# A work list and its loads, ordered anew from the value products of batch 2 on

## The chip, the cores and the metric

The kernel runs on one core of one Trainium2 chip. The metric is the device time of one execution in microseconds (us). Five engines work side by side, each on its own in-order queue: TensorE (PE, matrix products), VectorE (DVE), ScalarE (ACT), GpSimd (POOL) and SyncE (SP). An engine meets other engines' work only at semaphores. POOL, SP and ACT also issue DMAs, which move data while the engines go on.

## The reference

A causal attention over 8 batches, 8 heads, 576 queries and 64 channels, with 16 extra "beacon" keys and values that every query sees, and behind it a gated feed-forward block on the 4,608 rows that come out:

```python
scores = scale * np.matmul(q, k_all.transpose(0, 1, 3, 2))     # k_all: 16 beacons, then 576 keys
scores = np.where(causal, -1000000000.0, scores)
a = np.exp(scores - scores.max(-1, keepdims=True))
a /= a.sum(-1, keepdims=True) + 1e-09
x = np.matmul(a, v_all)                                        # then heads side by side: 4608 x 512
g = x @ w_gate
out = ((g * (1.0 / (1.0 + np.exp(-g)))) * (x @ w_val)) @ w_out   # d_ff = 1536
```

## The kernel before

Nothing is scheduled by a loop. One long string, `plan`, is the order of all work: each letter is one piece of work, `piece()` turns it into instructions on the engines concerned, and each engine takes its instructions in that order. The n-th letter of a kind is always the same piece, so a new order of letters changes only when a piece is issued. The list has 1,742 letters.

- `T`, `K`, `Q`: turn the keys and queries of batches 0 to 2 on PE and copy them into `kT` and `qT`.
- `l`: the next DMA load of the list `loads` (119 of them), issued by POOL. `vl[b][i]` is a chunk of the values of batch b (0: 16 beacon rows, 1: 112 rows, 2 to 4: 128 rows, 5: 80 rows), `kl[b][i]` the same for keys, `ql[b][i]` a chunk of queries (128 rows, the last 64). From the 25th on, a load first waits until PE has finished the last piece but one ahead of it (`passed[-2]`). `vb` and `qk` have two buffers each, taken by batch in turn. So a value load waits for the last value product of the batch two before, and a key or query load for the DMA transpose that read its place.
- `t`: one DMA transpose, issued by SP, from `qk` into `kT` or `qT` (batches 3 to 7, ten each: key chunk, query chunk, in turn). Written here as "the key transpose of batch 4, chunk 2".
- `S`: scores of one of four units A to D of a head pair on PE; `E`: the exponent on ACT; `D` or `M`: the causal mask of one unit, on DVE or on POOL.
- `P`, `p`: the value products of a head pair, first and second half, on PE; `R`: normalisation on DVE. "P 2.3" is batch 2, head pair 3.
- `V`: when the four head pairs of a batch are normalised, five or six DMA transposes on SP put them into `xT` (V 2 is that of batch 2).
- `G`, `H`: gate and value products of one of 12 column blocks of a chunk of 512 tokens on PE (16 matmuls in all); `a`: tanh on ACT; `1`, `2`: two operations on DVE that end in `hT`. There are nine chunks, j = 0 to 8; "G 2.0" is chunk 2, block 0. Chunk 2 needs V 2, chunk 3 needs V 3, and so on.
- `F`: output products on PE, 24 letters for 256 rows; `O` or `o`: the copy out of PSUM on DVE or ACT, and the store, which SP issues.

PSUM has four slots. A piece of PE that starts a new result takes the slot that has been free longest, and waits for the `E`, `2`, `R` or `O` that freed it. SP's queue holds the transposes `t` and `V` and the stores; POOL's holds loads and masks.

In the profile most PE work has line L151, the matmul in the helper `halves`; the full-height value products of batches 0 to 3 have L465; the DMA transposes are L320 (`t`) and L519 (`V`); loads are L202; exponents L379; masks L388 (DVE) and L392 (POOL).

Of the kernel before, what the change touches and what calls it, by code (L numbers as in the profile page):

```python
# [70 lines left out]
def kernel(  # L71
# [134 lines left out]
    def q_loads(b):  # L206
        return [lambda c=c, n=n: rows(natural(b, 0), q, b, c, 0, P * c, n) for c, n in enumerate((P, P, P, P, 64))]
# [455 lines left out]
    for i in range(2):  # L663
# [7 lines left out]
    vl = [v_loads(b) for b in range(B)]  # L671
    kl = [k_loads(b) for b in range(B)]
    ql = [q_loads(b) for b in range(B)]
# [17 lines left out]
    def piece(kind):  # L691
# [69 lines left out]
        "SH2EHDta1Gal2Gl1SH2ElHaMl1Gal2G1SH2ElHaDlG1a2lG1lSHE2HaMl1Ga2FFH1l2FaFlFF1FFFlF2FPplFRPlFFpVFlRF",
        "FFFFlFFFFFloFFFoFFlFFFFFFlSPESFlpEMSFRFESlFFFFEMDSFlFFEDSFFPlEGMoDpolGRHlGal1Hl2Ga1SlHE2HlaDG1al",
        "2G1SHEt2HaDt1Ga2Gt1SH2EtHMa1tGa2Gt1SH2EtHaD1Gta2G1tSH2EtHaDS1Pa2Ep1SlFEFRFFFlSFEF2VSFlFDFEFFMDSP",
        "ESlFpESFRMFEFlSFFESMDFFDlFFEDSFFFEMSFFFoMFFFoFFFESFFPEMSFtpEDGRMtGSHtEHMat1Ga2FtFH12Gta1Gt2HGta1",
        "Ht2Ha1Gta2FFH12Ga1G2FFFSFEFFFHOMGoaSHE1H2aDGa1G12H2SHaE1FFF2aFMP1Pp2pRFlSFEFFFRSlFESFFDPVlESDFpE",
        "MSFRlFFESFMFFElSFFFESMFFFOFElSFFOMFESMFFMFEDSFFFEMSFPEMFPpMpRGFRGHGa1H2Ha1Ga2FFH12Ga1G2HGa1H2Ha1",
        "Ga2FFH12Ga1G2HGa1H2Ha1Ga2FFF1SFEF2FHoDSOFaFFEF1SFF2EFSFDFFEDSFFPEMSFpEDSFRFESFFFDPEVMSFpEDSFREFS",
        "FFFEDMSFFOFESFDFFoFDFFESFFFEMSPFEDSpFERFMFFFFMFFFFFPOGOpGRHGa1H2Ga1H2Ga1H2Ga1H2Ga1PH2paGRH1VGa2H",
        "1G2a1FFFF2FHGa1H2Ha1Ga2FFH12FaFG1G2HGa1H2FaFFG1F2FFFFFFFFFFFFoFFFoFFFFFFFFHGa1FFFF2HGa1H2FaH1Ga2",
        "FF1G2FFFFHGa1H2FaHOGOa1G1H2Ha2G1a2G1H2Ga1FFFF2FFHGa1H2Ha1Ga2FFF1G2FFFHGa1FFH2Ha1Ga2FFH12Ga1G2FFF",  # L770
# [45 lines left out]
```

## Time and profile before

| what | value |
|---|---|
| median of 3 runs | 370.32 us (369.93 to 370.75) |
| the profiled execution | 369.36 us |
| its span, first to last instruction | 367.6 us |
| PE busy | 355.6 us, 97% |
| DVE, ACT, POOL busy | 227.1, 185.9, 124.6 us |
| granted TensorE clock, mean | 0.999 |
| DMA, mean over the span | 108 GB/s |

How to read it: spans are from the first to the last instruction, and the execution's own time is 1.76 us longer. Busy times of different engines overlap. Engines wait for each other through semaphores, and a wait in the profile is put down to whatever ended last before it; where that engine had long been done, it was something else. The chain of work that ended last goes back from the last instruction through whatever released each step.

### The profile page before, as it was taken

Reading aid. Unit: us, or ns where it says so; the run is one execution under the profiler, and the core shown is the slowest. Engines: PE = TensorE matmul, PEld = TensorE weight load, DVE = VectorE, ACT = ScalarE, POOL = GpSimd, SP = SyncE. Lnnn points to the kernel's source line nnn. Section 1 sums busy time; section 2 is a strip of 40 time slices with the busy share of each in tenths; the row PEclk is TensorE's granted clock in tenths of the full one; section 3 lists DMA queues with packets and bytes.
Section 4 is the critical chain, followed back from the end, with each engine's and each line's share of the span. In section 5 each row is a group of like instructions: output and inputs, shape, how many; then the busy total and the mean of one; then the engine's idle time right before and its main releaser. Section 6 shows DMA issues by size and latency. Waiting matters only on the chain.

```text
span 367.6 us, 11647 instructions
## 1 busy us (share of the span) xinstructions
PE 355.6 (97%) x5037; PEld 219.9 (60%) x5037; DVE 227.1 (62%) x429; ACT 185.9 (51%) x276; POOL 124.6 (34%) x201
## 2 busy tenths in 40 slices
PE   7799999989999999999999999999999999999996
PEld 3588565655565555555665567556766555555554
DVE  4577786548764676277636683767568735766631
ACT  3874688953576651736774458237913322322201
POOL 8862456972366286770350027000200000000000
PEclk9999999999999999999999999999999999999999
DMA  8999999999999999999598309301330201100113
GB/s 147 162 193 201 204 164 160 147 170 176 158 127 176 175 115 107 112 201 150 63 180 101 86 7 124 67 0 59 68 116 14 54 13 46 60 3 0 60 59 114
DMA packets 143988, 39.88 MB, mean 108 GB/s; under 512 B 130368, under 2 KB 139328, under 8 KB 143936
## 3 DMA queue, kind: packets, MB, share of 16 engines
q0 software_dynamic: 95424, 18.85, 73.0%
q1 hardware_dynamic: 48224, 19.92, 30.1%
q8 instruction: 39, 0.64, 0.7%
q10 hardware_dynamic: 288, 0.36, 0.3%
q14 instruction: 13, 0.11, 0.1%
HBM read 38.27 MB, written 9.44 MB: 130 GB/s over the span
## 4 chain that ended last, share of the span: by engine, by line
PE 88%; DMA 4%; DVE 3%; ACT 2%; issue 1%; POOL 1%; SPq 1%; POOLq 0%; ACTq 0%
PE gv_ps L151 51%; PE o_ps L151 23%; PE s_ps L151 6%; PE pv_ps L151 4%; PE pv_ps L465 4%; DMA xT<-x 2%; DMA qk<-in_q_dram 2%; PE t_ps L283 1%; ACT p L379 1%; DVE x L494 1%; SPq L519 1%; DVE x L427 0%; DVE kT L246 0%; POOL qk L193 0%; DVE p L388 0%
## 5 line engine op out<-in xcount | busy, mean ns | idle before, releaser
L151 PE MATMUL gv_ps<-xT,wg 64*128 64x512 bf16 (+2 forms) x912 | 196.0, 365 | 2.2 <-DVE p L388 1.9
L151 PE MATMUL gv_ps<-xT,wv 64*128 64x512 bf16 (+2 forms) x912 | 197.2, 365 | 0.0
L379 ACT ACTIVATE p<-s_ps 128x832 bf16<-128x832 f32 (+2 forms) x127 | 104.2, 867 | 36.8 <-PE s_ps L151 35.3
L551 ACT ACTIVATE th<-gv_ps 128x512 f32<-128x512 f32 (+2 forms) x114 | 65.5, 574 | 112.1 <-PE gv_ps L151 111.2
L151 PE MATMUL o_ps<-wo,hT 64*128 64x512 bf16 (+2 forms) x912 | 113.9, 365 | 0.2
L556 DVE SCALAR_TENSOR_TENSOR u<-th,gv_ps 128x512 f32<-128x512 f32 (+2 forms) x114 | 74.9, 657 | 59.3 <-ACT th L551 59.0
L151 PEld LDWEIGHTS <-wg 64*128 64x128 bf16 x912 | 83.9, 94 | 41.4 <-issue 1.9
L151 PEld LDWEIGHTS <-wv 64*128 64x128 bf16 x912 | 83.6, 94 | 35.2 <-issue 0.5
L563 DVE SCALAR_TENSOR_TENSOR hT<-gv_ps,u 128x512 bf16<-128x512 f32 (+2 forms) x114 | 75.2, 663 | 3.6
L151 PEld LDWEIGHTS <-hT 64*128 64x128 bf16 x912 | 46.7, 94 | 30.0 <-PE o_ps L151 1.2
L392 POOL TENSOR_SCALAR_AFFINE_SELECT p<-p 128x256 bf16<-128x256 bf16 (+2 forms) x66 | 25.3, 405 | 74.6 <-ACT p L379 72.3
L151 PE MATMUL s_ps<-qT,kT 64*128 64x336 bf16 (+3 forms) x512 | 45.0, 250 | 2.2 <-DVE kT L246 0.5
L202 POOL DMA_DIRECT2D vb<-in_v_dram x40 | 34.0, 854 | 22.7 <-PE gv_ps L151 15.9
L151 PEld LDWEIGHTS <-kT 64*128 64x128 bf16 x512 | 25.2, 94 | 21.9 <-DVE kT L246 1.2
L388 DVE TENSOR_TENSOR p<-p,upper 128x256 bf16<-128x256 bf16 (+2 forms) x77 | 21.4, 298 | 22.3 <-ACT p L379 21.2
L494 DVE TENSOR_TENSOR x<-pv_ps,rec 128x640 bf16<-128x640 f32 (+1 forms) x32 | 25.3, 791 | 1.2
L202 POOL DMA_DIRECT2D qk<-in_q_dram x25 | 21.3, 852 | 11.0 <-PE pv_ps L465 3.5
L246 DVE COPY o_sb<-o_ps 128x512 f32<-128x512 f32 (+2 forms) x22 | 14.0, 663 | 17.8 <-PE o_ps L151 12.8
L202 POOL DMA_DIRECT2D qk<-in_k_dram x25 | 21.1, 844 | 9.3 <-PE s_ps L151 3.9
L493 DVE RECIPROCAL rec<-pv_ps 128x10 f32<-128x10 f32 (+1 forms) x32 | 6.9, 215 | 24.2 <-PE pv_ps L151 16.2
L151 PEld LDWEIGHTS <-p 64*128 64x128 bf16 x960 | 18.4, 94 | 3.4 <-DVE x L494 0.2
L244 ACT ACTIVATE o_sb<-o_ps 128x512 f32<-128x512 f32 (+2 forms) x16 | 8.7, 570 | 22.5 <-PE o_ps L151 21.7
(63 smaller groups left out, 136.6 us busy)
## 6 DMA issues: line engine op xcount, KB each, us to landing
out_dram<-o_sb SPq DMA_DIRECT2D x34, 256.0 KB, 3.4
vb<-in_v_dram POOLq DMA_DIRECT2D x24, 128.0 KB, 7.1
qk<-in_q_dram POOLq DMA_DIRECT2D x20, 128.0 KB, 6.4
qk<-in_k_dram POOLq DMA_DIRECT2D x15, 128.0 KB, 6.8
wv<-in_moe_w_val_dram POOLq DMA_DIRECT2D x4, 384.0 KB, 8.9
wg<-in_moe_w_gate_dram POOLq DMA_DIRECT2D x4, 384.0 KB, 8.7
wo<-in_moe_w_out_dram POOLq DMA_DIRECT2D x2, 768.0 KB, 15.1
qk<-in_k_dram POOLq DMA_DIRECT2D x2, 576.0 KB, 13.4
```

The source lines that it names most:

```text
L151: ins = nc.tensor.matmul(o, lhsT=l, rhs=r, start=start, stop=stop)
L202: return nc.gpsimd.dma_start(dst[p0 : p0 + n, c, :, 0:D], src[b, :, r : r + n, :].rearrange("h j d -> j h d"))
L244: nc.scalar.activation(o, i, ACT.Copy)
L246: eng.tensor_copy(o, i)
L379: nc.scalar.activation(p_of(b, m, u == "A")[:, :, c0 : c0 + w], ps[:, :, 0:w], ACT.Exp, scale=0.125)
L388: nc.vector.tensor_tensor(out=ap, in0=ap, in1=upper[:, None, d : d + w].to_broadcast([P, 2, w]), op=ALU.mult)
L392: nc.gpsimd.affine_select(out=ap, in_=ap, compare_op=ALU.is_ge, fill=0.0, base=d, pattern=[[0, 2], [1, w]], channel_multiplier=-1,)
L465: ins = nc.tensor.matmul(o_ps[:, side, 68 * c : 68 * c + D + 1], lhsT=pt[n % NPT][:, side, col : col + P], rhs=vb[b % 2][:, t, 2 * m + sid ...
L494: nc.vector.tensor_tensor(out=xs[b][:, c0:NKT, P * m : P * m + P].rearrange("p c (h d) -> p h c d", d=D), in0=o[:, :, :, 0:D], in1=rec[:, ...
L551: nc.scalar.activation(th[:, 0:w], gvs[n][:, 0, 0:w], ACT.Tanh, scale=0.5)
L556: nc.vector.scalar_tensor_tensor(out=u[:, 0:w], in0=ths[n][:, 0:w], scalar=1.0, in1=gvs[n][:, 0, 0:w], op0=ALU.add, op1=ALU.mult)
L563: nc.vector.scalar_tensor_tensor(out=hTs[j][:, f, c0:c1], in0=gvs.pop(n)[:, 1, 0 : c1 - c0], scalar=0.5, in1=ths.pop(n)[:, 0 : c1 - c0], o ...
```

## The change

Up to letter 380 of the list (PE reaches it at 72.4 us) and up to the 54th load nothing is changed. Behind it the remaining 1,362 letters and 65 loads are put into a new order. The counts of every kind stay, with one exception: one causal mask moves from POOL (`M`) to DVE (`D`).

What moves, in the order of the list:

- P 2.3 and p 2.3 stand right behind P 2.2 and p 2.2 and ahead of the gate products of chunk 1, instead of behind them.
- V 2 stands between the transposes of batch 3 and those of batch 4, instead of behind those of batch 4. Chunk 2's gate and value products follow chunk 1's at once, and the 48 output letters of rows 512 to 1023 come behind them instead of ahead.
- The value products of batch 3 move from there to behind chunk 2, in pairs: P 3.0 with P 3.1, P 3.2 with P 3.3.
- The remaining loads are mixed over batches and kinds. Three early ones of the values of batches 4 and 3 and the end of batch 4's keys and queries go first, then none over more than 20 gate and value letters, and then 14 in close order, which begin with `ql[6][4]` and end with `vl[3][4]` and `vl[3][5]`.
- From there on stages keep their order, with value products, stores and transposes shifted by some letters. At the end, the last four copies out of PSUM swap engines two and two (`Oo` and `oO`).

```diff
@@ -678,11 +678,11 @@
         run_loads(2)[1], run_loads(2)[0], vl[2][5], ql[3][0], vl[1][5], kl[3][1], vl[1][3], lambda: load_wo(1),
         kl[3][2], vl[2][4], vl[2][3], vl[2][0], vl[2][2], vl[2][1], kl[3][0], ql[3][1], kl[3][3], ql[3][2],
         kl[3][4], ql[3][3], kl[3][5], ql[3][4], kl[4][0], kl[4][1], ql[4][0], kl[4][2], ql[4][1], kl[4][3],
-        ql[4][2], kl[4][4], ql[4][3], kl[4][5], ql[4][4], vl[3][0], vl[3][1], vl[3][2], vl[3][3], vl[3][4],
-        vl[3][5], kl[5][0], kl[5][1], ql[5][0], kl[5][2], ql[5][1], kl[5][3], ql[5][2], kl[5][4], ql[5][3],
-        kl[5][5], ql[5][4], vl[4][0], vl[4][1], vl[4][2], vl[4][3], vl[4][4], vl[4][5], kl[6][0], kl[6][1],
-        ql[6][0], kl[6][2], ql[6][1], kl[6][3], ql[6][2], kl[6][4], ql[6][3], kl[6][5], ql[6][4], vl[5][0],
-        vl[5][1], vl[5][2], vl[5][3], vl[5][4], vl[5][5], kl[7][0], kl[7][1], ql[7][0], kl[7][2], ql[7][1],
+        ql[4][2], kl[4][4], ql[4][3], vl[4][3], vl[3][0], vl[4][4], kl[4][5], ql[4][4], ql[6][4], kl[6][4],
+        vl[4][1], vl[3][2], vl[3][1], vl[3][3], vl[4][2], kl[5][1], ql[5][0], ql[6][3], vl[4][5], kl[5][0],
+        vl[3][4], vl[3][5], ql[5][3], kl[6][2], ql[6][0], kl[5][5], ql[6][1], ql[5][1], kl[5][2], vl[5][0],
+        kl[6][1], ql[5][4], kl[5][3], kl[5][4], kl[6][5], vl[5][1], vl[4][0], kl[6][0], ql[5][2], kl[6][3],
+        ql[6][2], vl[5][2], vl[5][3], vl[5][4], vl[5][5], kl[7][0], kl[7][1], ql[7][0], kl[7][2], ql[7][1],
         kl[7][3], ql[7][2], kl[7][4], ql[7][3], kl[7][5], ql[7][4], vl[6][0], vl[6][1], vl[6][2], vl[6][3],
@@ -754,22 +754,22 @@
         "lqKGlQSlHElGDa1lSHE2HaD1Gal2SHE1s2aFFFDESF1FFEls2EDSlTETlKlTKqlTDqKlksQEQSESPEDpSRPEplDSRESlFFFD",
-        "ESlFDFFEDSPlpEDlsRFEFSlFFDFElSPEDtlpSlRFESFtFlFFDESDFFVlFEDFSOFFlESOFFFlESPplESRFFlESFFFElSFFFEM",
-        "SFFFMESFMFFMESFtMDFFESPMDtMpoDPEOlpRlSGEtlRMGtDHlGat1Ht2Gal1Ht2Gat1Hl2Gta1Ht2lGa1Ht2Gat1H2Gtla1H",
-        "t2Ga1StHE2HMat1Gal2tG1SHt2EHaDl1SFaFFl2EFFF1SFMESF2FFlFEDSFPEMpPDlRpSFEFRVSFFFESlFDFFESlFFFESFMF",
-        "OlFESFFOFMFESPlEpSlRFESFFMFMFDESlFtPEMDpSRFtMESFlFFEFMDGtDGtSHEtFFaMGl1tFF2FFFtSHOEHaMtol1Ga2G1t",
...
+        "ESlFDFFEDSPlpEDlsRFEFSlFFDFElSPEDtlpSlRFESFtFlFFDESDFFVlFEDFSOFFlESOFFFlESPplESRFFlESFFFElSFMMFM",
+        "FESMFFMDFESFtMFMESFFFEMtSPOpEMOSREMPtpDRPptRGltGlHtGat1H2Gat1H2VGal1Hl2Gal1H2Ga1H2Ga1SHtE2HaDtG",
+        "1a2tG1SHEt2HaDt1Ga2Gt1SH2EtHaMtG1a2Gt1SHE2tHaD1Ga2G1SH2EHMa1Gla2Gl1SlH2ElHal1Ga2lG1lSH2ElHalG1al",
+        "2G1MSHME2lHaDl1Gal2Gl1SHl2EHDal1SFaFF2lEFFF1SFlESF2FlFFDEFPMpMPRplSFRlEFSFFEFFDSFESMFtFFFEDSFFOF",
+        "EFSFDFoMFFFESFtFFEDSFPtEMpPRMptSlFREFSFlFEFFDVSlFEFDFFFSMFESlFOFFFEOSlFFDFEFlFFFlFSFESMDFFFFEMFF",
...
```

More of the change, by code (lines that the diff above doesn't have):

```diff
@@ L761 @@
[L761 to L770, printed above, removed]
@@ L771 @@
-        "FFFFFFOFFFHOGa1H2Ha1Ga2FFH12Ga1FFFF2FFHFaFFF1FFFF2FFFFFOFFFFOFFFFFFFFFFFFFFFFFFFFoFFOFFFFFFFFFOo",
-        "FFFFFFFFFFFFoO",
+        "ESlFDFFEDSPlpEDlsRFEFSlFFDFElSPEDtlpSlRFESFtFlFFDESDFFVlFEDFSOFFlESOFFFlESPplESRFFlESFFFElSFMMFM",
+        "FESMFFMDFESFtFMFESMFFFEMtSPOpEMOSREMPtpDRPptGRltGlHtGat1H2Gat1H2VGal1Hl2Gal1H2Ga1H2Ga1SHtE2HaDtG",
+        "1a2tG1SHEt2HaDt1Ga2Gt1SH2EtHaMtG1a2Gt1SHE2tHaD1Ga2G1SH2EHMa1Gla2Gl1SlH2ElHal1Ga2lG1lSH2ElHalG1al",
+        "2G1MSHME2lHaDl1Gal2Gl1SHl2EHDal1SFaFF2lEFFF1SFlESF2FlFFDEFPMpMPRplSFRlEFSFFEFFDSFESMFtFFFEDSFFOF",
@@ new lines @@
+        "EFSFDFoMFFFESFtFFEDSFPtEMpPRMptSlFREFSFlFEFFDVSlFEFDFFFSMFESlFOFFFEOSlFFDFEFlFFFlFSFESMDFFFFEMFF",
+        "FFlFFMFtFoFlFFOFFFlFFFGlGlHlGa1FlFH2lHa1Gtla2FFF1tG2FFtFPFFptFRFFHtGa1H2FaHOGOa1Gl2H1lGa2Hl12Gal",
+        "1SHEl2HaDlG1a2Gl1SHlE2HaDl1SFaFlF2EFFF1SlFEtP2FMFpMtFRFFSPEtFSpMESFRtFEFSFFDPEDtSFpEDStFRlFESMFF",
+        "FEDVSlFFFoFDPloFFpElSFRFESFMFFlESFPMESFplESFRFMFFEMFFMFDSFtESFPEFMtSpFEDGRtGOHDoGat1H2Gta1Ht2Ga1",
+        "Ht2Gat1SHE2tHMa1Gat2G1tSH2EHtaD1Gat2G1StH2EHaDG1a2G1SHE2HaM1FaSFF2EFFF1SMFESF2FFFEMSFPEDFFpMSFRl",
@@ new lines @@
+        "ESFFFEFDVSlFFESDPlFFEpMFRFloFSFoFFDlFESFFFEDlSFFFEDSPFFEMpSFRMESFFFEMFSFFESMFFFGEDOGMoHGa1H2Ga1H",
+        "2Ga1H2Ga1H2Ga1H2Ga1H2Ga1H2Ga1H2Ga1H2Ga1H2Ha1FaFFF2FFF1FFP2FFpFRPFSpESFRFESFFFDVEMFFFFFDFFOSFESFF",
+        "FFoMFFFESFFEMFSPEDFSpFEDSFRFFESFFDPEDSFpEMSFRFEMPFFDpoGRGOHGa1H2Ga1H2Ga1H2Ga1H2Ga1PH2paGRH1VGa2H",
+        "1G2a1H2Ga1H2Ga1H2FaFH1FaF2FFF1FFG2GHGa1H2FaFFG1F2FFFFFFFFFFFFOFFFFoFFFFFFFHGa1H2Ha1Ga2FFH12Ga1G2",
+        "FFFHGa1H2Ha1Ga2FFH12Ga1G2FFFFFFOFFFFOFHGa1H2Ha1Ga2FFH12Ga1G2HGa1FH2FaFG1FH2Ga1H2Ha1Ga2FFF1G2FFFF",
@@ L773 @@
+        "FFHGa1H2FaFFG1oHO2Ga1FFFF2FFFFFFFFHFaFFF1FH2FaFFF1FFFF2oFFFoFFFFFFFFFFFFFFFFFFFFFOFFOFFFFFFFFFoO",
+        "FFFFFFFFFFFFOo",
     ]
```

## The prediction

> **What bounds the kernel now.** I read the page's busy row and granted clock first, then PE's waits, then PE and SP in order of time at the places where PE stood still, and last how long DMAs take to land.
>
> ```profile
> span 367.6 us, 11647 instructions
> PE 355.6 (97%) x5037; PEld 219.9 (60%) x5037; DVE 227.1 (62%) x429; ACT 185.9 (51%) x276; POOL 124.6 (34%) x201
> ...
> PEclk9999999999999999999999999999999999999999
> ...
> PE 88%; DMA 4%; DVE 3%; ACT 2%; issue 1%; POOL 1%; SPq 1%; POOLq 0%; ACTq 0%
> ```
>
> PE is the bound and its clock is full, so a new order can only win back PE time that is lost now, or lose some. From 80 to 360 us the ten-us stretches show PE at 9.8 to 10.0 of 10, but for one with 9.49. PE's waits name two losses in the changed part:
>
> ```profile
> PE gv_ps L151 <- DVE p L388: 1.9, 2, 1.4
> ...
> PE gv_ps L151 <- DMA xT<-x: 0.2, 1, 0.2
> ```
>
> PE in order of time, at 77.5, 116 and 155 us:
>
> ```profile
> 77.51 0.35 PE L151 MATMUL s_ps<-qT,kT 64*128 64x336 bf16 x4
> 79.24 0.37 PE L151 MATMUL gv_ps<-xT,wg 64*128 64x512 bf16 x1 [1.38 <-DVE p L388]
> ...
> 116.96 0.37 PE L151 MATMUL gv_ps<-xT,wg 64*128 64x512 bf16 x1 [0.51 <-DVE p L388]
> ...
> 155.44 0.37 PE L151 MATMUL gv_ps<-xT,wg 64*128 64x512 bf16 x1 [0.19 <-DMA xT<-x]
> ```
>
> The reader should see that all three are first gate products of a chunk (G 1.0, 2.0, 3.0). A mask is no input of a gate product, so "DVE p" is not the cause. The landings of V 1's, V 2's and V 3's last needed piece are at 79.11, 116.71 and 155.31 us, each 0.13 to 0.25 us ahead: all three waited for a V transpose. Counted from starts of matmuls, against what their letters take elsewhere, PE loses 1.55, 0.67 and 0.36 us there, and 0.38 us round 178 us (value products of batch 4). The rest behind 72.4 us are some 0.1 us at each change between half-height and full-height value products (two a block, five blocks) and the tail. So about 3 us can be won at most.
>
> SP in order of time, where the transposes of batch 3 and 4 go out, and PE's first reading of batch 3's last one:
>
> ```profile
> 80.11 1.51 SPq L320 DMA_TRANSPOSE kT<-qk  x1
> 81.71 2.75 SPq L320 DMA_TRANSPOSE qT<-qk  x1
> 84.57 1.34 SPq L320 DMA_TRANSPOSE kT<-qk  x1
> 86.00 1.92 SPq L320 DMA_TRANSPOSE qT<-qk  x1
> 88.00 1.29 SPq L320 DMA_TRANSPOSE kT<-qk  x1
> 89.39 1.23 SPq L320 DMA_TRANSPOSE qT<-qk  x1
> ...
> 103.59 1.20 SPq L320 DMA_TRANSPOSE qT<-qk  x1
> 105.93 2.55 SPq L519 DMA_TRANSPOSE xT<-x  x2
> ...
> 98.39 0.36 PE L151 MATMUL s_ps<-qT,kT 64*128 64x336 bf16 x4
> ```
>
> SP is back to back from 73.6 to 104.8 us. It is behind the list there, and nothing suffered: the transpose of 89.39 landed at 97.46, and its reader, S 3.0B, came at 98.39.
>
> **The change part by part.** I put PE's letters of the new list end to end from 72.4 us, by rows: 0.86 for a G or H ("0.86 ... x8"), 0.216 for an F ("0.65 ... x6"), 0.16 to 0.20 for an S, 0.45 for a P or p. I call this list time. The sum of PE work is the same in both lists; only waits differ.
>
> *P 2.3 ahead of G 1.0.* G 1.0 still needs V 1, which is issued before the change, so 79.1 us stays. The hole of 1.55 is filled with 0.91 of work. POOL's masks for batch 2 run from 73.68, ten by 77.3 in the trace, and three more (0.42, 0.35, 0.45) now precede P 2.3's end, so to 78.5. The last exponent comes right behind its scores at about 77.9 (the copy of 0.60 that held ACT at 75.6 goes to DVE), its DVE mask at 78.25. P 2.3 and p 2.3 end at 79.1, G 1.0 goes at 79.25. PE then stands 0.85 behind list time instead of 1.74. Gain 0.9; bounds 0.4 (masks late by 0.5) and 1.1.
>
> *Batch 3's value products in pairs.* Four blocks of full-height products instead of five: gain 0.19.
>
> *V 2 early.* List time from V 2 to G 2.0 is 15.2 us instead of 9.6. V 2 starts at 88.5 to 90.7 (below); its fourth piece is issued 3.9 later and lands 4 to 7 on, by 96.5 to 101.6, against 100.5 for G 2.0. Gain 0.67; bounds 0 and 0.67.
>
> *V 3.* 9.7 us of list time from V 3 to G 3.0 in both lists, with fewer loads beside it (544 rows of loads in ten us instead of 832). Of 0.36 I take 0.2 as won; bounds -0.4 and 0.36.
>
> *Batch 3's transposes against S 3.0B.* In the new list S 3.0B comes at list time 94.1, so at 94.95: 3.4 us earlier than now. SP's sequence up to the transpose it reads is the same, only with fewer loads in flight (416 instead of 656 rows between 77 and 89 us). If SP goes as in the trace, it lands at 97.46 and PE waits 2.5. If SP's long issues (2.75, 1.92) shrink to 1.4, it goes out at 87.5 and lands by 94: no wait. I take 0.5, near the second end.
>
> *V 2's cover, the transposes of batch 4.* V 2's five issues (6.57 us in the trace) now stand ahead of the ten of batch 4. The first load behind the pause, `ql[6][4]`, overwrites what the last query transpose of batch 4 reads. List time gives it 5.3 us behind that transpose; it was over 12. It is due at 107.8 + 0.85 = 108.65. The transpose itself is the twentieth behind the one at 80.1. At 1.25 apiece (shortest row 1.19, and a gap) it goes out at 105.1 and lands 2.8 later, 107.9. At 1.42, the mean of batch 4's, 108.5 and 111.7. As in the trace (23.5 for fifteen, and V 2) 110.1, landing up to 6 later. I take the middle, 112, a little above since the first six run among loads: POOL stands still for 3.3 us.
>
> *What is queued behind.* On POOL twelve more loads stand between `ql[6][4]` and `vl[3][5]`, which P 3.0's last matmul needs. Back to back they take 0.87 (128 rows), 0.82, 0.72, 0.69 or 0.52 each in the trace. With two masks (0.36, 0.42) `vl[3][5]` starts 11.3 us after `ql[6][4]`. List time gives 17.3 us from one to P 3.0's last matmul, so 6.0 us less the stop are left for landing. The value loads of 80 rows landed in 5.0 to 7.3 us behind 90 us; of all value loads from 78 to 152 us the trace says:
>
> ```profile
> DMA to landing us min/median/max: 2.8/5.9/12.4
> ```
>
> I take 5.0, the lowest of its size, since SP is idle by then. So P 3.0 waits the stop less 1.0. A wait at S 3.0B shortens the stop by as much; both together are 112 - 108.65 - 1.0 = 2.35, taken as 0.5 and 1.85. Bounds 0 (first case) and 6 (last).
>
> One page gives another figure for a load. By the Trainium skill, page "DMA: Bandwidth & Descriptors", section "Anatomy of one DMA", a GpSimd DMA takes about 2.0 us and its bytes at 436 GB/s, for 82 KB an estimate of 2.2 us; by it P 3.0's wait would be gone and the sum near 369.2. The trace shows no value load of this size under 4.98 us, so the sum goes by the trace.
>
> *V 4.* SP gets six transposes of batch 6 right ahead of it (6 x 1.42 from list time 173.1: 181.6). Its third piece landed 8.1 after its start before: 189.7 against G 4.0 at 190.2. Loss 0.2; bounds 0 and 1.5.
>
> *Edits at no cost.* Stores move with the F letters (the first from 107 to 130), off SP's full stretch. One mask more on DVE costs 0.3 us of an engine that is idle 38%. Output letters behind chunk 2 need `hT` buffers that are free long before. From 121.6 to 146.2 ACT has 18.3 us of work in 24.6 and DVE 12.0; from 171.4 to 190.2 ACT has 17.5 in 18.8 (15.4 before), which covers its slots but barely: if a slot is late there, 0.2 to 0.4 appears, as round 178 now, so I leave that 0.38 as it is. V 5 and V 6 get 0.6 and 1.1 us more room, V 7 the same. The last two copies of 128 columns swap engines: DVE's ended at 364.84, ACT's at 364.79, so one store goes 0.05 earlier and one 0.05 later.
>
> **Sum.** -0.9 - 0.19 - 0.67 - 0.2 + 0.5 + 1.85 + 0.2 = +0.6 us. The profiled execution took 369.36, 0.96 below the median of the three; added to the median it is 370.9, and since the large unknown, SP, has its far end at +4, I put it at 371.1.
>
> **Rivals.**
>
> 1. SP keeps up. With fewer loads its issues go at 1.25, S 3.0B and P 3.0 don't wait: 371.1 - 2.35 = 368.75. For it: issues of 1.19 to 1.27 fill most rows behind 90 us. Against: one in six takes 1.8 to 2.2 even in quiet stretches.
> 2. The loads land faster when nothing else moves, in 3.5 us, as the quickest full ones at 130 to 147 us: P 3.0 waits 0.35, and the time is 369.6. The page named above speaks for it too.
> 3. SP runs as in the trace. S 3.0B waits 2.5, POOL stands still for longer, P 3.0 waits 1 to 3: 372.5 to 375, say 373.4. For it: the same fifteen transposes took 23.5 us. Against: 240 rows of loads less beside them. From an SP pitch of 1.5 on this decides.
> 4. The hole at 77.5 isn't filled, since POOL, now with all but two of batch 2's late masks, holds P 2.3 until 79: 371.6.
>
> **How the numbers follow.** Two tenths of a per cent, 0.74 us, is about what can be told from no change. The forecast, 371.1, has 0.43 (its own range 370.2 to 372.2: 0.23 slower, 0.20 same). Rival 3 has 0.20, all slower; rival 4 0.08 (0.05 slower, 0.03 same); rival 1 0.17, faster; rival 2 0.12, half faster, half same. So faster 0.23, same 0.29, slower 0.48. The range goes from rival 1 to rival 3: 368.4 to 373.9.
>
> **What would show it.** In the changed kernel G 1.0 goes at about 79.25 behind p 2.3, and G 2.0 without a wait near 101. PE should stand still twice that it doesn't now: at S 3.0B near 95 us for a landing in `qT`, and in P 3.0 near 126 for a load into `vb`. POOL should wait some 3 us near 109 for a transpose. I am wrong if PE shows no wait at P 3.0, if SP's issues between 80 and 110 us average under 1.3 or over 1.6, or if a wait over 1 us stands behind 150 us.

## The result: 1.0% slower, and the profile after

| what | before | changed |
|---|---|---|
| median, runs side by side | 370.06 us (368.25 to 373.03, 15 runs) | 373.51 us (371.19 to 376.57, 15 runs) |
| ratio | | 1.010, 95% interval 1.0075 to 1.0126 |
| the profiled execution, its span | 369.36, 367.6 us | 373.96, 372.2 us |

The ratios here and below leave out runs more than 1.5% above the fastest of their kernel, which the medians and ranges keep, and the profiled executions of two experiments (378.51 us with batch 3's scores later, 376.35 with the new list up to V 2) are such runs.

The change costs some 3.5 us, where 0.8 was forecast. The page of the changed kernel: the busy row of PE, its share by slices, the granted clock by slices, the queue that brings instructions, and the chain.

```profile
span 372.2 us, 11639 instructions
PE 357.2 (96%) x5037; PEld 206.3 (55%) x5037; DVE 226.7 (61%) x432; ACT 187.0 (50%) x276; POOL 122.8 (33%) x198
...
PE   8699999999899999999799999999999999999996
...
PEclk9999999999999999999899999999999999999999
...
q8 instruction: 39, 0.64, 0.7%
...
PE 88%; DMA 4%; ACT 2%; DVE 2%; issue 1%; SPq 1%; POOL 1%; POOLq 0%; ACTq 0%
```

The twentieth slice (176.8 to 186.1 us) falls out of both rows: PE is busy for seven tenths of it, and its clock is not full. Before, neither was so. The 8 in the eleventh (93 to 102 us) is the stop at S 3.0B, below. PE's waits of the changed kernel:

```profile
PE s_ps L151 <- issue: 2.4, 1, 2.4
PE t_ps L283 <- DMA qk<-in_q_dram: 2.1, 2, 1.8
PE s_ps L151 <- DMA qT<-qk: 1.6, 1, 1.6
```

The third line is a wait that the prediction has. The first is not in it. The second lies in the unchanged part (10.57 to 12.33 us); it is the main reason why this execution came to letter 380 1.0 us later than the one of before, so places up to S 3.0B are compared with that 1.0 taken off.

PE of the changed kernel in order of time, at four places that matter:

```profile
79.36 0.93 PE L465 MATMUL pv_ps<-vb,p 128*128 128x65 bf16 x25 [0.23 <-DVE p L388]
80.22 0.39 PE L151 MATMUL gv_ps<-xT,wg 64*128 64x512 bf16 x1
...
97.70 0.36 PE L151 MATMUL s_ps<-qT,kT 64*128 64x336 bf16 x4 [1.61 <-DMA qT<-qk]
...
180.11 0.62 PE L151 MATMUL pv_ps<-vb,p 64*128 64x65 bf16 x30
180.56 0.36 PE L151 MATMUL s_ps<-qT,kT 64*128 64x336 bf16 x3
183.27 0.23 PE L151 MATMUL s_ps<-qT,kT 64*128 64x128 bf16 x1 [2.35 <-issue]
```

G 1.0 goes right behind p 2.3: the hole is filled. S 3.0B (97.70) waits for the transpose. At S 5.0C PE stops for 2.35 us in the middle of one unit: three of its matmuls are done, the fourth, which reads the same unit's tiles, comes only at 183.27. "Issue" means that the profile shows nothing that PE waited for.

From letter 380 to the start of its last matmul PE takes 295.39 us, against 291.88 before: 3.51 more. Counted as in the prediction (starts of matmuls against what their letters take elsewhere), it goes here:

| place | change of the loss, us |
|---|---|
| hole at 77.5, less the 0.40 that P 2.3 now waits for a mask | -1.15 |
| G 2.0 | -0.67 |
| G 3.0 | -0.36 |
| S 3.0B | +1.77 |
| S 5.0C | +2.52 |
| the letters behind S 5.0C, at half clock | +1.6 |

These sum to 3.7. The rest, 0.2 less, lies in small differences, among them the 0.38 that before lost round 178 us and the changes between half-height and full-height products, eight instead of ten.

**The stop at S 5.0C.** PE's instructions come in blocks: queue q8 moved 0.64 MB in 39 packets, 16 KB each. PE has 10,074 matmuls and weight loads and some 40 other instructions, so a block holds about 256 (the experiment that shifts the blocks, below, has it exactly). DMA in two stretches of the changed kernel, 177.2 to 180.4 us and 180.4 to 182:

```profile
DMA packets 3123, 0.51 MB, mean 160 GB/s; under 512 B 3123, under 2 KB 3123, under 8 KB 3123
...
q0 software_dynamic: 2114, 0.27, 137.8%
q1 hardware_dynamic: 1009, 0.25, 57.0%
...
q0 software_dynamic: 982, 0.12, 128.3%
q1 hardware_dynamic: 451, 0.11, 87.9%
q8 instruction: 1, 0.02, 5.7%
```

In the first stretch loads (q0) and transposes (q1) move 3,123 packets, and no instruction block comes. The block comes in the second, from 180.48 to 181.94 us. PE began the last instruction that it had at 180.70 and the next at 183.26, 1.32 us behind the end of the packet. Over the whole trace the blocks follow PE's instruction count: a fetch never starts earlier than some 290 instructions ahead of the end of what PE has. How long 290 instructions last depends on what they are. PE and its clock in windows of time, before and then changed; the columns are length, busy time and count of each engine, granted clock, DMA share, GB/s:

```profile
174.25:177.75 3.50, 3.50 (x42) 2.03 (x39) 2.81 (x6) 1.92 (x3) 0.00 (x0) 1.00 0.89 102
```

```profile
177.00:180.80 3.80, 3.80 (x149) 2.92 (x142) 1.98 (x5) 2.13 (x3) 2.05 (x6) 1.00 1.99 163
180.60:184.00 3.40, 1.05 (x21) 0.57 (x15) 1.20 (x3) 0.98 (x2) 0.45 (x2) 1.00 1.67 117
184.00:187.40 3.40, 3.40 (x74) 2.81 (x72) 0.58 (x2) 2.18 (x3) 0.00 (x0) 0.50 0.18 37
187.40:190.80 3.40, 3.40 (x76) 2.50 (x72) 1.53 (x4) 2.94 (x5) 2.23 (x5) 1.00 0.27 43
```

The new list puts the half-height value products of P 4.1 and P 4.2 close together: 149 matmuls and 142 weight loads in 3.8 us, where the stretch of before holds 42 and 39 in 3.5 us. So 290 instructions last 3.81 us here, the shortest behind 100 us; before, the shortest was 4.53. And in the same stretch the list has batch 7's key and query loads beside batch 6's transposes: the block came 5.05 us behind the earliest moment it could be asked for. Fetches as long as that exist before too (6.15 us at 155 us, 5.26 at 165), but with 12 us of instructions in hand. 5.05 us to the end of the packet and 1.32 from there to PE's next instruction are 6.37, against 3.81 in hand: 2.56 us missing, and 2.52 lost. In the five traces that have such a stop, PE goes on 1.32 to 1.41 us behind the end of the packet. The last rows show what follows it: 3.4 us at a clock of 0.50.

### The profile page after: what moved, and what is told of

Same layout as the page of the kernel before. It is cut to its first block, busy times and chain, and to the rows that moved or that the text cites. A ratio compares the mean times of both kernels' runs of the same rounds, so it can differ in the third digit from the quotient of the medians.

```text
span 372.2 us, 11639 instructions
## 1 busy us (share of the span) xinstructions
PE 357.2 (96%) x5037; PEld 206.3 (55%) x5037; DVE 226.7 (61%) x432; ACT 187.0 (50%) x276; POOL 122.8 (33%) x198
## 4 chain that ended last, share of the span: by engine, by line
PE 88%; DMA 4%; ACT 2%; DVE 2%; issue 1%; SPq 1%; POOL 1%; POOLq 0%; ACTq 0%
PE gv_ps L151 47%; PE o_ps L151 25%; PE s_ps L151 6%; PE pv_ps L151 4%; PE pv_ps L465 4%; DMA qT<-qk 2%; DMA qk<-in_q_dram 2%; PE t_ps L283 1%; ACT p L379 1%; SPq L320 1%; DVE x L427 0%; DVE kT L246 0%; POOL qk L193 0%; ACT kT L244 0%; ACT th L551 0%
## 5 line engine op out<-in xcount | busy, mean ns | idle before, releaser
L151 PE MATMUL gv_ps<-xT,wv 64*128 64x512 bf16 (+2 forms) x912 | 195.2, 365 | 0.0
L151 PEld LDWEIGHTS <-hT 64*128 64x128 bf16 x912 | 42.8, 94 | 32.4 <-PE o_ps L151 1.2
L392 POOL TENSOR_SCALAR_AFFINE_SELECT p<-p 128x256 bf16<-128x256 bf16 (+2 forms) x63 | 23.6, 401 | 87.1 <-ACT p L379 87.0
L151 PEld LDWEIGHTS <-kT 64*128 64x128 bf16 x512 | 24.3, 94 | 27.2 <-issue 6.0
L151 PEld LDWEIGHTS <-p 64*128 64x128 bf16 x960 | 20.0, 96 | 4.7 <-issue 0.6
L151 PE MATMUL pv_ps<-vb,p 64*128 64x65 bf16 x960 | 21.0, 193 | 0.0
```

Source lines behind the costliest of these rows:

```text
L151: ins = nc.tensor.matmul(o, lhsT=l, rhs=r, start=start, stop=stop)
L392: nc.gpsimd.affine_select(out=ap, in_=ap, compare_op=ALU.is_ge, fill=0.0, base=d, pattern=[[0, 2], [1, w]], channel_multiplier=-1,)
```

## The experiments

Each is compared with the kernel before on the same chip: 369.91 us for the first four, 370.25 for the next four, 370.67 for the last three.

### Batch 3's scores one place later

The letters `S` and `E` of S 3.0B to S 3.0D and a mask go behind later pieces (two rows of the list):

```diff
-        "1a2tG1SHEt2HaDt1Ga2Gt1SH2EtHaMtG1a2Gt1SHE2tHaD1Ga2G1SH2EHMa1Gla2Gl1SlH2ElHal1Ga2lG1lSH2ElHalG1al",
-        "2G1MSHME2lHaDl1Gal2Gl1SHl2EHDal1SFaFF2lEFFF1SFlESF2FlFFDEFPMpMPRplSFRlEFSFFEFFDSFESMFtFFFEDSFFOF",
+        "1a2tG1Ht2Hat1Ga2Gt1SH2EtHaMtG1a2Gt1SHE2tHaD1Ga2G1SH2EHMa1Gla2Gl1SlH2ElHal1Ga2lG1lSH2ElHalG1al2G1",
+        "MSHME2lHaDl1Gal2Gl1SHl2EHDal1SFaFF2lEFFF1SFlESF2FlFSFDEFEPMpMDPRplSFRlEFSFFEFFDSFESMFtFFFEDSFFOF",
```

> The changed list with batch 3's scores moved: the score, exponent and mask letters of S 3.0B leave their place behind G 1.9 and one set is added behind F 2.9, so that every unit of batch 3 from 3.0B on comes one place (about 3.5 us of PE work) later. Theory A (S 3.0B waits for the landing of batch 3's last query transpose, which SP issues at 89.4 whatever PE does): the wait of 1.77 us before S 3.0B goes (0 to 0.3 left), nothing takes its place, and the time falls by 1.0 to 1.8 us against the changed kernel (373.5), to about 372. Rival (SP or the slots move with PE, so the wait only moves): S 3.0B or S 3.0C waits 1 us or more, time within 0.5 us of the changed kernel. The stop of 2.4 us at S 5.0C stays by both.

Measured: 373.64 us (371.52 to 378.51), ratio 1.011 (1.0075 to 1.0145). S 3.0B no longer waits, and nothing is won. PE in order of time in P 3.0:

```profile
130.18 0.31 PE L465 MATMUL pv_ps<-vb,p 128*128 128x65 bf16 x5 [0.83 <-DMA vb<-in_v_dram]
132.60 0.58 PE L465 MATMUL pv_ps<-vb,p 128*128 128x65 bf16 x14 [2.11 <-DMA vb<-in_v_dram]
```

P 3.0 now waits, 3.28 us in all, for value loads. The wait at S 3.0B had hidden this one: P 3.0 came 54.9 us behind letter 380 in the changed kernel and comes 53.5 behind it here, while its last load goes out no earlier. The stop at S 5.0C stayed, at 3.2 us of "issue", in this trace without a half clock behind it.

### Batch 7's key and query loads 8 to 10 us earlier

Eleven letters `l` move up in the list; nothing else changes:

```diff
-        "FFlFFMFtFoFlFFOFFFlFFFGlGlHlGa1FlFH2lHa1Gtla2FFF1tG2FFtFPFFptFRFFHtGa1H2FaHOGOa1Gl2H1lGa2Hl12Gal",
-        "1SHEl2HaDlG1a2Gl1SHlE2HaDl1SFaFlF2EFFF1SFlEtP2FMFpMtFRFFSPEtFSpMESFRtFEFSFFDPEDtSFpEDStFRlFESMFF",
+        "FFlFFMFtFoFlFFOFFFlFFFGlGlHlGa1FlFH2lHa1Gtla2FFFl1tG2lFFtFlPFlFptFlRFFlHtGa1Hl2FalHOGlOa1lG2Hl1G",
+        "a2H12Ga1SHE2HaDG1a2G1SHE2HaD1SFaFF2EFFF1SFEtP2FMFpMtFRFFSPEtFSpMESFRtFEFSFFDPEDtSFpEDStFRlFESMFF",
```

> The changed list with the eleven loads of batch 7's keys and queries moved up by 8 to 10 us of list time, to start right behind the last value load of batch 5; PE's order is untouched. Theory B (PE stops at S 5.0C because its next 16 KB of instructions, 256 of them, come through DMA engines that are full of these loads and of batch 6's transposes; and a stop of that length is followed by 3.4 us at half clock): the block that is fetched at 180.5 to 181.9 now is fetched 1.5 us or more earlier against PE, the stop at S 5.0C falls from 2.4 to under 0.8 us, no half clock in mid-run, time 3 to 4.5 us under the changed kernel (369 to 370.5). Rival C (S 5.0C waits for batch 5's transposes or another semaphore): the loads compete with batch 5's transposes instead, the stop stays at 2 us or more, time within 1 us of the changed kernel or above it.

Measured: 371.73 us (369.02 to 375.16), ratio 1.0032 (1.0002 to 1.0062). The same instructions pass S 5.0C, with all four of its matmuls in one row:

```profile
182.82 0.36 PE L151 MATMUL s_ps<-qT,kT 64*128 64x336 bf16 x4
```

The fetch of the block that was late starts 1.24 us behind its earliest moment instead of 3.59. The time is above the 369 to 370.5 expected: here too P 3.0 waits (1.97 us lost), since S 3.0B didn't, and a half clock window follows it. So the stop, and the half clock with it, is about two thirds of the slowdown: the ratio falls from 1.010 to 1.003.

### 112 more PE instructions ahead of S 3.0B

This shifts every later block boundary by 112 instructions and leaves order and loads as they are. 56 matmuls of 4 columns are added to the computation:

```diff
+        if n == 49:
+            src = below[:].rearrange("p g n -> p (g n)")
+            for _ in range(28):
+                for row in range(2):
+                    r = slice(HALF * row, HALF * row + HALF)
+                    nc.tensor.matmul(ps[:, row, 0:4], lhsT=src[r, 0:P], rhs=src[r, 0:4], start=True, stop=True)
```

> The changed kernel with 56 tiny extra matmuls (4 columns, with their weight loads 112 instructions of PE) ahead of S 3.0B, into PSUM that S 3.0B then overwrites. Order, loads and waits are untouched; only where PE's blocks of 256 instructions begin is shifted by 112. The matmuls take about 0.8 us and lie in the wait of 1.77 us that S 3.0B has. Theory B (PE runs dry at S 5.0C since 290 instructions, from the request of a block to the end of the one before, take only 3.8 us there): the dense stretch falls elsewhere in its block, the least time for 290 instructions up to 230 us is 5.6 us, the stop and the half clock go, time 3 to 4.5 us under the changed kernel. Rival C (S 5.0C waits for data): stop and half clock stay, time 0 to 1 us above the changed kernel.

Measured: 373.44 us (371.68 to 374.44), ratio 1.0087 (1.0055 to 1.0119). The stop at S 5.0C is gone, and another of 1.56 us stands a few pieces behind it, in the middle of p 4.3:

```profile
186.10 0.32 PE L151 MATMUL pv_ps<-vb,p 64*128 64x65 bf16 x9 [1.56 <-issue]
```

That settles what PE waits for. Instructions that PE has begun when it stops (matmuls, weight loads and 21 others), counted in the traces: 5,057 in the changed kernel, 5,057 with the scores moved, 5,313 here, exactly 256 more. A wait for data would have stayed at its letter. The time is not the 3 to 4.5 us lower that I expected: the next block is late as well, and P 3.0 waits here (1.88 us in one stop) where S 3.0B doesn't.

### Before, with six stops of growing length

Dummy masks on POOL hold PE up at six places of the kernel before, to see what brings the half clock:

```diff
+    def stop(k):
+        after(nc.gpsimd.nop(), newest[0], "stop")
+        for _ in range(k):
+            ins = nc.gpsimd.affine_select(
+                out=scratch[:], in_=scratch[:], compare_op=ALU.is_ge, fill=0.0, base=0, pattern=[[0, 2], [1, P]],
+                channel_multiplier=-1,
+            )
+        after(nc.tensor.nop(), ins.ins.name, "stop")
...
+    stops = {1248: 1, 1431: 2, 1476: 3, 1533: 4, 1579: 5, 1629: 7}
```

> The kernel before with six stops of PE, where it otherwise runs through: at six letters from 236 us on PE waits for 1, 2, 3, 4, 5 and 7 operations of 0.42 us on POOL that start when PE's work ahead is done, so stops of about 0.7, 1.1, 1.5, 2.0, 2.4 and 3.2 us, 11 us in sum. Theory D (the clock halves for some 3.4 us after PE has stood still for longer than a threshold between 1.7 and 2.35 us): the first three cost their own length, the last two a further 1.7 us each, the fourth decides; time about 370 + 11 + 3.4 to 5. Rival (the half clock at 184 us had another cause): granted clock full everywhere but at the end, time 381.

Measured: 385.32 us in a single execution. The stops came out at 0.54, 1.02, 1.56, 2.04, 2.51 and 3.46 us. Half clock followed the 2.04 and the 3.46, each time for 3.41 us, and not the 2.51. The same windows view, around the 2.04 and the 2.51:

```profile
313.84:317.25 3.41, 1.37 (x14) 0.50 (x12) 2.67 (x4) 0.76 (x2) 1.63 (x4) 1.00 0.00 0
317.25:320.67 3.42, 3.42 (x20) 1.20 (x16) 0.00 (x0) 0.00 (x0) 0.00 (x0) 0.50 0.00 0
330.90:334.30 3.40, 1.47 (x14) 0.49 (x10) 1.51 (x3) 0.60 (x1) 1.59 (x4) 1.00 0.00 0
334.32:337.73 3.41, 2.85 (x28) 1.31 (x30) 0.28 (x1) 0.60 (x1) 0.43 (x2) 1.00 0.00 0
```

The clock changes only at multiples of 3.413 us from one another within an execution (here 11 such steps lie between the two half clocks). Laid on that grid, the 2.04 falls into one window whole, which is 1.37 us busy; the 2.51 is cut in two, 1.95 and 0.56. So the length of a stop doesn't decide, but how much of it falls into one window. Two stops at S 5.0C agree: the 3.22 us with the scores later are cut into 1.75 and 1.48, the 2.53 with the value loads ahead (below) into 1.44 and 1.09, and no half clock follows either.

### The new list up to V 2, the old order behind it

Letters up to 470 and 59 loads are new; what is left follows in the old order (the first rows behind the join):

```diff
-        "FESMFFMDFESFtFMFESMFFFEMtSPOpEMOSREMPtpDRPptGRltGlHtGat1H2Gat1H2VGal1Hl2Gal1H2Ga1H2Ga1SHtE2HaDtG",
...
+        "FESMFFMDFESFtFMFESMFFFEMtSPOpEMOSREMPtpDRPptGRltGlHtGat1H2Gat1H2VGal1Hl2Gal1H2Ga1H2Ga1lllttlttH2",
+        "Gtla1Ht2Ga1StHE2HMat1Gal2tG1SHt2EHaDl1SFaFFl2EFFF1SFMESF2FFlFEDSFEMPDlpSFEFRSFFFESlFDFFESlFFFESF",
...
```

> The new list up to letter 470 (P 2.3 early, V 2 early, chunk 2 right behind chunk 1), and behind it what is left in the old order, loads too. My theory (the losses are the waits at S 3.0B and P 3.0, the late instruction block at S 5.0C and the half clock behind it, and all of them lie behind letter 470): what is left is the gain at 77.5 (0.9) and at G 2.0 (0.67), so 1.5 us faster than before, some 368.5 against 370.0 us, with no stop over 1 us behind 80 us. Rival (the early value products or V 2 themselves cost time elsewhere, for instance through batch 4's transposes going out later): 370 us or more, with a stop behind 100 us that before does not have.

Measured: 373.92 us (369.76 to 376.62), ratio 1.0067 (1.0032 to 1.0101). My theory fell here. PE stood still ahead of S 4.0B:

```profile
119.83 0.53 PE L151 MATMUL s_ps<-qT,kT 64*128 64x336 bf16 x4 [4.69 <-issue]
```

This "issue" is no late block (one had come at 115.50, 11 us ahead of need). The transpose that the unit reads went out at 111.90 on SP and landed at 119.73, by the records of the transposes. How many of the twelve runs stop for so long isn't shown: the two fastest (369.76 and 370.32 us) have a mean granted clock of 1.0, and in this trace two half clock windows come with the stop. SP's row for V 2 is

```profile
90.37 7.68 SPq L519 DMA_TRANSPOSE xT<-x  x5
```

and batch 4's ten transposes stand behind it. The old order needs them at S 4.0B, ahead of G 2.0, so the rival held. So V 2's early place is no gain by itself: SP's time is taken from batch 4. The new list can afford it since it starts batch 4's scores 18 us later (133.3 us in the changed kernel, 114.9 before).

### Value loads ahead of POOL's wait

In the changed kernel `ql[6][4]` and `vl[3][4]` change places, `kl[6][4]` and `vl[3][5]` too:

```diff
-        ql[4][2], kl[4][4], ql[4][3], vl[4][3], vl[3][0], vl[4][4], kl[4][5], ql[4][4], ql[6][4], kl[6][4],
+        ql[4][2], kl[4][4], ql[4][3], vl[4][3], vl[3][0], vl[4][4], kl[4][5], ql[4][4], vl[3][4], vl[3][5],
...
-        vl[3][4], vl[3][5], ql[5][3], kl[6][2], ql[6][0], kl[5][5], ql[6][1], ql[5][1], kl[5][2], vl[5][0],
+        ql[6][4], kl[6][4], ql[5][3], kl[6][2], ql[6][0], kl[5][5], ql[6][1], ql[5][1], kl[5][2], vl[5][0],
```

> The changed kernel, but the first two loads behind the pause and the last two of that group of 14 change places: vl[3][4] and vl[3][5] first, ql[6][4] and kl[6][4] last. My theory: P 3.0 can no longer wait, since its last values are loaded before POOL stands still for batch 4's last query transpose; S 3.0B may still wait (0 to 1.8 us), and the stop at S 5.0C with the half clock behind it stays (up to 4 us together): 371 to 373, about 1 us faster than the changed kernel where P 3.0 waits there. Rival (P 3.0's wait comes from the landing times of the loads, not from their place in POOL's queue): the same time as the changed kernel, P 3.0 waiting 1 to 2 us.

Measured: 374.63 us (372.2 to 378.81), ratio 1.011 (1.0072 to 1.0147). No gain, above what I expected. P 3.0 didn't wait, but neither did it in the changed kernel's profile: S 3.0B (1.53 idle) and S 5.0C (2.53) both stood.

### Both edits of the loads, and then the scores too

The first of these two joins the earlier loads of batch 7 with the value loads ahead; the second adds the later scores. The edits are the diffs above.

> Both edits of the loads: batch 7's key and query loads 8 to 10 us earlier (as in the run that took the stop at S 5.0C away and stood at a ratio of 1.003) and vl[3][4], vl[3][5] ahead of the wait for the transpose. My theory: no stop at S 5.0C, no wait in P 3.0, S 3.0B 0 to 1.8: the total loss of PE behind 72 us is 3 to 5 us, the time 368.5 to 370, so the same as before or up to 0.4% faster. Rival (a loss spread over the new order, not these stops, makes it slower): 371 us or more though none of the three stops is there.

> As the run with both edits of the loads, and batch 3's scores from S 3.0B on one place later. My theory: S 3.0B does not wait either, and since P 3.0's values are there early the wait cannot move to it as it did when the scores alone were moved: total loss of PE behind 72 us 3 to 4 us, the time 368.3 to 369.5, no slower than the run without it. Rival (the two waits are one and the same lateness, and whatever comes behind chunk 2 pays it): a stop of 1 us or more appears at the next piece that needs a load or a transpose of batch 4, and the time is that of the other runs.

Measured: 370.62 us (367.69 to 372.21), ratio 1.0001 (0.9975 to 1.0027), with S 3.0B waiting 2.39 us as the one stop left (0 to 1.8 and 368.5 to 370 us were expected); and with the scores moved 368.50 us (367.27 to 372.72), ratio 0.9964 (0.9933 to 0.9995). The second is faster than the changed kernel, and than the one before by 0.4%, with an interval that ends just under 1. Its page:

```profile
span 366.4 us, 11638 instructions
...
PE   8799998999999999999999999999999999999996
...
PEclk9999999999999999999999999999999999999999
```

No wait over 0.5 us stands behind 80 us, and from letter 380 to its last matmul PE takes 289.95 us, against 291.88 before. Its DMA queues from 174.9 to 178.5 us, the stretch that answers to 177 to 181 of the changed kernel:

```profile
q1 hardware_dynamic: 1385, 0.34, 53.0%
q8 instruction: 1, 0.02, 2.4%
```

Without loads beside it the packet ends 1.23 us ahead of the moment at which 290 instructions are used up. PE's next instruction comes 1.37 us behind the packet, so it is still 0.14 us late.

### The early value products alone

The new list up to letter 433 (P 2.3 in the hole, V 2 not moved), the old order behind it; three loads of batch 3's values then stand close together:

```diff
-        "SFFFMESFMFFMESFtMDFFESPMDtMpoDPEOlpRlSGEtlRMGtDHlGat1Ht2Gal1Ht2Gat1Hl2Gta1Ht2lGa1Ht2Gat1H2Gtla1H",
...
+        "FESMFFMDFESFtFMFESMFFFEMtSPOpEMOSREMPtpDRPptGRltGlllHlGa1Ht2Gal1Ht2Gat1Hl2Gta1Ht2lGa1Ht2Gat1H2Gt",
...
```

> The new list only up to letter 433, so with P 2.3 and p 2.3 in the hole at 77.5 us and V 2 not yet issued; behind it the old order, loads too. My theory (the hole is filled for 0.9, and what cost 4.85 us at S 4.0B with the cut at 470 was V 2 ahead of batch 4's transposes): no stop at S 4.0B, G 2.0 waits some 0.7 us for V 2 as before, the time 0.9 us below before, 369.2 (368.6 to 369.8). Rival (the early value products themselves push something back): a stop over 0.5 us between 100 and 125 us that before does not have, 370 us or more.

Measured: 371.30 us (368.88 to 375.86), ratio 1.0012 (0.9982 to 1.0042): no difference that shows. The hole is filled (from letter 380 to G 1.0 it takes 6.80 us, as in the changed kernel, with 0.91 of work more in it than the 6.83 of before). But G 2.0 takes the gain back. PE's waits:

```profile
PE gv_ps L151 <- DMA xT<-x: 2.3, 2, 1.9
```

V 2 is the end of SP's chain of transposes, which does not move when PE gets there sooner. Only with V 2 early does the hole at 77.5 pay. The rival's stop is there in size, but at G 2.0 and not for its reason.

### Each of the other two edits taken back

From the version at 368.50 us: once `vl[3][4]` and `vl[3][5]` behind POOL's wait again, once batch 7's loads late again.

> As the run with both edits of the loads and the later scores, which took 368.5 us, but vl[3][4] and vl[3][5] again last of their 14 loads, behind POOL's wait. My theory (without a wait at S 3.0B the wait in P 3.0 is there in full): P 3.0 waits 1.5 to 3 us, half clock behind it in part of the runs: 370 to 372.5. Rival (the place of the two loads does not matter): 368.5.

> As the run that took 368.5 us, but batch 7's key and query loads where the changed kernel has them. My theory: PE stops at S 5.0C for 1 to 3 us with no data late, and where the stop leaves 2.0 us or more idle inside one 3.41 us clock window the next window is at half clock: 370 to 372.5, the stop alone in the trace behind 80 us. Rival (the stop needs the lateness that the other two waits bring): 368.5.

Measured: 371.18 us (369.72 to 376.34), ratio 1.0025 (0.9988 to 1.0061), and 373.13 us (371.48 to 376.99), ratio 1.0071 (1.0042 to 1.0099). POOL of the first in order of time, and then PE:

```profile
114.04 0.69 POOL L202 DMA_DIRECT2D qk<-in_q_dram  x1 [5.48 <-DMA qT<-qk]
...
124.79 1.64 POOL L202 DMA_DIRECT2D vb<-in_v_dram  x2
```

```profile
128.36 0.31 PE L465 MATMUL pv_ps<-vb,p 128*128 128x65 bf16 x5 [0.88 <-DMA vb<-in_v_dram]
130.64 2.69 PE L465 MATMUL pv_ps<-vb,p 128*128 128x65 bf16 x46 [1.98 <-DMA vb<-in_v_dram]
```

This is the prediction's chain in full: POOL stands still for batch 4's last query transpose, the two value loads go out from 124.79 on, and P 3.0 waits. Of the second, which lies above the 370 to 372.5 expected, PE in order of time, and then its windows:

```profile
183.81 0.28 PE L151 MATMUL s_ps<-qT,kT 64*128 64x128 bf16 x1 [3.67 <-issue]
```

```profile
182.95:186.36 3.41, 2.54 (x17) 1.62 (x19) 0.29 (x1) 1.54 (x2) 0.00 (x0) 0.50 0.57 94
186.36:189.78 3.42, 3.42 (x76) 2.94 (x74) 1.03 (x3) 1.48 (x3) 0.00 (x0) 0.50 0.00 0
```

PE stops again behind its 5,057th instruction, with no other wait over 0.5 us behind 80 us: the stop needs no earlier lateness. Here two windows run at half clock.

All eight combinations of the three edits have been run (medians, us):

| batch 7's loads | value loads | scores in place | scores later |
|---|---|---|---|
| late | behind the wait | 373.51 (the changed kernel) | 373.64 |
| late | ahead | 374.63 | 373.13 |
| earlier | behind the wait | 371.73 | 371.18 |
| earlier | ahead | 370.62 | **368.50** |

Batch 7's loads are worth 1.8 us alone. Moving the scores is worth 1.5 to 2.1 where the value loads are ahead, and within 0.6 of nothing where they are not. From 368.50, taking back the scores costs 2.1, the value loads 2.7, batch 7's loads 4.6 (before stood 0.4 higher beside the last two). The profiled executions divide the same way: with batch 7's loads late all four stop at S 5.0C (2.35, 3.22, 2.53 and 3.67 us), with them earlier none does. From the earliest moment for the block at this place to the end of its packet, 2,858 to 3,485 packets of loads start in the first four and none in the others; this takes 5.05 to 6.35 us in the first four and 2.25 to 2.58 in the others.

## Why the prediction was right and wrong

The direction was right and the time is inside the range, in part by luck. The forecast of 371.1 was 2.4 us low. Rival 3, at 373.4, is close by the number: its condition, SP as in the trace, came true, but the waits that it forecast from it cost 1.77 us, half of what the change lost. Without the stop and the half clock at S 5.0C, 2.5 and 1.6 us, PE's stretch in the profile would be no longer than before. What the forecast did weigh is better seen with batch 7's loads earlier: 1.0032, where 1.002 was forecast.

**Right.** *P 2.3 ahead of G 1.0*: 0.9 forecast. With the 1.0 us of the start taken off, G 1.0 goes at 79.2 (79.25 forecast), 0.94 us better against the list. *V 2 early*: G 2.0 doesn't wait; V 2 starts at 90.65 and has landed by 99.58, inside the bounds. *Batch 3's value products in pairs*: eight switches of some 0.1 us instead of ten. *V 3*: 0.36 won where 0.2 was taken. *V 4*: no loss at G 4.0, where 0.2 was taken. POOL's wait for batch 4's last query transpose: 3.18, where 3.3 was taken (below). SP's issues from 80 to 110 us average 1.44, inside the 1.3 to 1.6 named.

**Nearly right in sum, wrong in its parts.** *Batch 3's transposes against S 3.0B* and *What is queued behind*: 0.5 and 1.85, "both together" 2.35. In the changed kernel's profile all of it was at S 3.0B: 1.77, and P 3.0 did not wait, which the prediction had named as a sign of being wrong. The sum is near since two terms missed in opposite ways.

At S 3.0B, 0.5 was too little. SP took 2.73 and 1.94 us for the same two transposes as before, and the last one landed at 97.56, where it had landed at 97.46. So the case with a wait of 2.5 came, not the one that 0.5 was near to; that PE was 1.0 us late in this execution took part of it away. In P 3.0, 1.85 was too much. POOL in order of time there:

```profile
113.82 0.69 POOL L202 DMA_DIRECT2D qk<-in_q_dram  x1 [3.18 <-PE gv_ps L151]
```

The view names PE here, but the wait is the one for the transpose. The transpose landed at 113.26, and POOL's own semaphore instruction for it was released at 113.28; the piece of PE that the load waits for (H 2.3) had ended at 110.67. In the run with the two value loads behind the wait again, landing (113.48) and load (114.04) lie as close, and there the view names the transpose. `vl[3][5]` went out at 124.98, 11.2 us behind `ql[6][4]` (11.3 forecast). What was wrong is its landing: 3.25 us, where 5.0 was taken, and so it was there 0.5 us ahead of P 3.0's last matmul. That is rival 2's mechanism.

In four traces without a wait at S 3.0B (scores later, batch 7's loads earlier, 112 more instructions, value loads behind the wait again) P 3.0 came sooner, the same load took 3.3 to 4.9 us, and P 3.0 lost 1.97 to 3.28 us. So the trade between the two waits is shown. Rival 1 fell, since SP did not get faster, and so did rival 4: P 2.3 waited 0.40 for a mask, and the hole is filled.

**The step that failed.** *Edits at no cost.* It weighed ACT's and DVE's slots between 171 and 190 us and left the 0.38 round 178 us as it was. The resource that ran out there was none of these: it was PE's own instructions. P 4.1 and P 4.2 next to each other use them up faster (290 in 3.81 us), and batch 7's loads, in the same stretch, make a block come later (5.05 us, and 1.32 more until PE goes on). The sum should have had +2.5 there. With it went the first sentence on the bound, that PE's "clock is full": the stop brings a half clock window, +1.6 in the profile. The sum was +0.59. With 2.52 and 1.62 added, 0.58 taken off since S 3.0B and P 3.0 lost 1.77 instead of 2.35, 0.36 for V 3 and V 4, which lost nothing, and 0.37 for the loss round 178 us, which is gone, it is 3.42, against the 3.51 measured. The prediction named its own test for this, a wait over 1 us behind 150 us, and it is met.

On blocks, the Trainium skill, page "Runtime: NRT & Kernel Launch", section "Instruction fetch mechanics", says that an engine fetches its instructions in 16 KiB blocks of 256 by a DMA queue of its own, and that the cost of crossing a boundary is mostly hidden. The trace agrees on size and count (39 packets, 0.64 MB, stops 256 apart); "mostly" leaves out the case here, 2.35 to 3.67 us of PE at one boundary in four traces.

How often the half clock comes goes with the spread of the times. A window of 3.41 us at half clock takes 0.0046 off the mean granted clock of an execution. Of the changed kernel's 15 runs, five have a mean clock of 0.998 or more, as without such a window: 371.95 us on average. Eight are at 0.994 or 0.995, as with one: 374.4 on average. Two are at 0.990 and 0.991, as with two: 376.2. So about 2 of the 3.5 us are there without any half clock (waits and stop, less the gains). The rest goes with the clock; that longer stops bring both is likely, but these runs have no trace. Of the runs of before beside the experiments, 63 of 82 have 0.998 or more.

What stays open: that the loads in flight delay the block is shown by moving them alone; how they do it, and whether the transposes beside them add to it, was not tried. Nor is it shown what fills the 1.3 us from the end of the packet to PE's next instruction. And each trace is one execution: with the same list up to there, S 3.0B waited 1.77 us in the changed kernel and not at all in the run with batch 7's loads earlier.

## What to carry to other kernels

When work is reordered on an engine that is already full, count its instructions per microsecond as well as its time, and look at what moves over DMA where they are densest: a stretch of many small matmuls beside heavy loads ran out of instructions here, and the profile then showed a wait for "issue" at a letter that had nothing to do with it. (Another wait for "issue" in this case was a transpose that landed late, so the name alone doesn't decide.) To tell it from a wait for data, shift the instruction count and see whether the stop stays at its letter. Two waits in a row can hide each other, so mend them together and measure the combinations: here three edits were worth at most 1.8 us alone and 5 together.

## What the runs showed of the hardware

- PE's instructions come in blocks of 256, and PE stopped at one and the same count (5,057 begun) in four kernels (the changed one, scores later, value loads ahead, batch 7's loads late again), and at 5,313 with 112 instructions added. It went on 1.32 to 1.41 us behind the end of the late packet in all five.
- The half clock comes in windows of 3.413 us on a grid that is fixed within an execution. Behind 80 us and ahead of the tail, each window with 2.04 us or more without a matmul was followed by a half clock window (idle of 2.04, 2.24, 2.35, 2.18, 2.04, 2.86, 2.81 and 3.41 us). Windows with 1.95, 1.75, 1.61 and 1.56 were not. Among value products it came after 1.64 in one run and not after 1.62 in another, and in the unchanged start it came after 1.4 in two runs and not in others, and after 1.9 in one and not after 1.8 in another, so idle time alone is not the whole measure. A window that was itself at half clock was followed by another where it held 0.86 or 1.01 us of idle.
- The Trainium skill, page "TensorE: Matmul & The Clock Gate", section "What's actually happening", has the free-running window of 3,413 ns and the two clocks, with half speed after at least one idle window. The traces agree on the window and on 0.50 and 1.00; 2.04 us of idle in a window, six tenths of it, were enough here.
